# Moving a pair's products behind a step's first product, and x's forms one step behind the norm

## Chip, cores, metric

One core of a Trainium2 chip. The metric is device time in microseconds, the median of several executions. A trace records the clock granted to TensorE. Up to the last matmul it is 1.00 except in stretches of 3.41 us, or two of them in a row, at 0.50; these are called half-clock windows here, and cold windows in the recorded texts.

## The reference

Linear attention on 8 batches x 8 heads x 576 x 64, an RMS norm, then a two-layer block on 4608 tokens with 512 inputs and 2048 hidden units:

```
kv  = einsum('bhsd,bhse->bhde', k, v)
out = einsum('bhsd,bhde->bhse', q, kv)
x   = out / sqrt(mean(out*out, -1) + 1e-6) * g_norm     # -> (4608, 512)
h   = x @ w_in
g   = h * erf(softplus(h))
y   = g @ w_out
```

## The kernel before

Tokens go in groups of 512. The first two groups use plain fp32 matmuls while the weights are brought into fp32 (group 0) and cut into three forms (the "upper" one made by ScalarE, the two "lower" ones by VectorE) that are stored to HBM (group 1). That takes the first 280 us. The other groups use the three forms, and there TensorE is full. The first two groups make 32 steps; step n makes one 128-row slice of h (`h_ps`, 4 matmuls, each run as two) and projects the slice of step n - 5 (`o_ps`). The attention of the next group is cut into pieces, four steps to a pair of heads, and dealt out over the steps. In the traces VectorE, ScalarE and TensorE's matmuls run in the order of the program.

```python
def products():                      # cut
    kv_ps = ...                      # 12 matmuls of k and v; VectorE copies them to bd (block-diagonal)
    qt_ps = ...                      # 4 transposes of q
    nc.scalar.copy(st["qT"], qt_ps)
def apply():                         # cut
    nc.tensor.matmul(kv_ps[:, o_tail], lhsT=bd, rhs=tail, ...)
    nc.tensor.matmul(o_ps, lhsT=bd, rhs=qT, ...)          # se_ps in the profile
    nc.scalar.activation(qT, o_ps, AF.Square)
def halve(): ...                     # VectorE: square into two parts
def mean():  ...                     # TensorE 2 matmuls, ScalarE Ln, Exp, Square (2 table loads)
def norm():  ...                     # VectorE, 3 instructions; reads ms_ps, then se_ps
def split(): ...                     # x into 3 forms: ScalarE one ("upper"), then VectorE two
# the four PSUM tiles of a pair share two banks, so norm must free them for the next products

def pieces_of(T):
    steps = [([], []) for _ in range(FC + 1)]
    for p in range(NP):
        *four, norm, split = attention(T, p)
        for i, piece in enumerate(four):
            step = BATCH * p + i
            if T == 1 and p == 0:
                step = min(i + 1, 3)
            late_in = 0
            if T == FIRST and p == NP - 1 and i == 3:
                step, late_in = step - 1, 1
            steps[step][late_in].append(piece)
        if T == FIRST and p == NP - 1:
            steps[FC - 1][0].extend((norm, split))
        else:
            steps[BATCH * p + BATCH][0][:0] = [norm, split]
    return steps

for n in range(FIRST * FC + 1):      # cut
    for piece in steps[f][0]: piece()
    weights()                        # group 0: weight conversion, 2 ScalarE + 5 VectorE instructions
    # VectorE: hs[n-4] *= ss[n-4]  (the gate)
    # TensorE: h_ps;  ScalarE: copy to h, Softplus
    # group 1: VectorE lowers three weight tiles and stores them, ScalarE uppers two more
    # every 4th step: Erf of four slices on ScalarE, with two table loads
    for piece in steps[f][1]: piece()
    # group 1: third weight upper
    project(n - LAG)                 # TensorE: o_ps
```

Of the kernel before, what the change touches and what calls it, by code (L numbers as in the profile page):

```python
# [49 lines left out]
BATCH = 4  # L50
LAG = 5

FIRST = 2
# [4 lines left out]
def kernel(  # L58
# [17 lines left out]
    NP = H // 2  # L76
    KC = DM // P
    FC = DF // P
# [25 lines left out]
    def softplus_table():  # L104
        nc.scalar.preload_act_table_set("softplus")  # L105
# [137 lines left out]
    def weights():  # L243

        w_next("split")
        w_next("join")
        w_next("load")
# [192 lines left out]
    def w_upper(which, f):  # L440

        t = stage.tile([P, 3, G], FP32R, name="w_new", tag="w_new")
        if which == "in":
            x, parts = w_in_sb[:, :, f * P : f * P + P], t.rearrange("p i (c f) -> p i c f", c=KC)
        else:
            x, parts = w_out_sb[:, f, :], t
        upper_w(x, parts[:, 0])
        w_new[which, f] = t, x, [parts[:, i] for i in range(3)]

    def w_lower(which, f):  # L450
        t, x, parts = w_new.pop((which, f))
        lower_w(x, *parts)
        kept = w_kept[which, f] = dram.tile([P, 3, G], FP32, name=f"w_{which}{f}")
        nc.sync.dma_start(out=kept, in_=t.bitcast(FP32))
# [5 lines left out]
    def project(f, g, last):  # L460
        for j in range(J):
            if f == 0:
                o_ps[j] = ps_o.tile([P, DM], FP32, name=f"o_ps{j}", tag=f"o{j}")
            nc.tensor.matmul(  # L464
                o_ps[j],
                lhsT=g[:, j * P : j * P + P],
                rhs=w_out_sb[:, f, :],
                start=(f == 0),
                stop=last,
            )  # L470

    def store(T, j, e):
        if T < B:
            rows = out[T * S : T * S + G, :].rearrange("(p j) f -> p j f", j=J)
            nc.sync.dma_start(out=rows[:, j, :], in_=e)
            return
        for h, side in enumerate((nc.sync, nc.scalar)):
            first_row = (2 * j + h) * S + G
            side.dma_start(out=out[first_row : first_row + R, :], in_=e[h * R : h * R + R, :])
# [3 lines left out]
    def sums():  # L483

        for j in range(J):
            e = es[j] = acc.tile([P, DM], FP32, name="e", tag="e")
            if j % 2:
                nc.scalar.copy(e, o_ps[j])
            else:
                nc.vector.tensor_copy(out=e, in_=o_ps[j])  # L490

    def unit(name):
        return gate.tile([P, G], FP32, name=name, tag=name[0])
# [28 lines left out]
    def load_parts(which, n):  # L522

        pool = w_in_p if which == "in" else w_out_p
        for _ in range(n):
            if w_seq[which]:
                key = w_seq[which].pop(0)
                t = pool.tile([P, 3, G], FP32, name=f"w_{which}_parts", tag="w")
                nc.sync.dma_start(out=t, in_=w_kept[key])
                w_now.setdefault(key, []).append(t)  # L530


    def pieces_of(T):


        steps = [([], []) for _ in range(FC + 1)]
        for p in range(NP):
            *four, norm, split = attention(T, p)
            for i, piece in enumerate(four):
                step = BATCH * p + i  # L540
                if T == 1 and p == 0:

                    step = min(i + 1, 3)
                late_in = 0
                if T == FIRST and p == NP - 1 and i == 3:
                    step, late_in = step - 1, 1
                steps[step][late_in].append(piece)
            if T == FIRST and p == NP - 1:
                steps[FC - 1][0].extend((norm, split))
            else:  # L550
                steps[BATCH * p + BATCH][0][:0] = [norm, split]
        return steps

    to_cut = [(which, f) for which in ("in", "out") for f in range(FC)]
# [2 lines left out]
    for n in range(FIRST * FC + 1):  # L557
        T, f = divmod(n, FC)
        if n == FC:
            early_room.close()  # L560
            late = ctx.enter_context(tc.tile_pool(name="late", bufs=1))
            x_new = ctx.enter_context(tc.tile_pool(name="x_new", bufs=1))
            acc = ctx.enter_context(tc.tile_pool(name="acc", bufs=J))
            stage_room = ctx.enter_context(ExitStack())
            stage = stage_room.enter_context(tc.tile_pool(name="stage", bufs=5))
            x_forms[FIRST] = late.tile([P, 3, KC, G], FP32R, name="x_forms0")
        if T < FIRST:
            if f == 0:
                ends = steps[FC][0] if T else []
                steps = pieces_of(T + 1)  # L570
                steps[0][0][:0] = ends
            for piece in steps[f][0]:
                piece()
        while w_at["join"] < len(w_order) and w_order[w_at["join"]][0] <= n + 1:
            weights()
        done = n - LAG + 1
        if 0 <= done < whole:
            nc.vector.tensor_tensor(out=hs[done], in0=hs[done], in1=ss[done], op=ALU.mult)
        if T < FIRST:
            h_ps = ps_h.tile([P, G], FP32, name="h_ps", tag="h")  # L580
            for c in range(KC):
                nc.tensor.matmul(  # L582
                    h_ps,
                    lhsT=w_in_sb[:, c, f * P : f * P + P],
                    rhs=xT[T][:, c, :],
                    start=(c == 0),
                    stop=(c == KC - 1),
                )
            if n == whole:
                old_h = wide.tile([P, BATCH, G], FP32, name="h", tag="h")  # L590
            h = hs[n] = old_h[:, n - whole] if n >= whole else unit("h_sb")
            s = ss[n] = unit("s_sb")
            nc.scalar.copy(h, h_ps)
            nc.scalar.activation(s, h, AF.Softplus)
            for key in list(w_new):
                w_lower(*key)
            if T == FIRST - 1:
                for key in to_cut[:2]:
                    w_upper(*key)
                if not w_new and stage_room is not None:  # L600
                    stage_room.close()
                    stage_room = None
                    w_in_p = ctx.enter_context(tc.tile_pool(name="w_in_p", bufs=BATCH))
                    load_parts("in", BATCH)
            if f % BATCH == BATCH - 1:
                for i in range(n - BATCH + 1, n + 1):
                    nc.scalar.activation(ss[i], ss[i], AF.Erf)
                softplus_table()
            for piece in steps[f][1]:
                piece()  # L610
            if T == FIRST - 1:
                for key in to_cut[2:3]:
                    w_upper(*key)
                del to_cut[:3]
        if n >= LAG:
            T2, f2 = divmod(n - LAG, FC)
            last = n - LAG in (FC - 1, whole - 1)
            project(f2, hs[n - LAG], last)
            if last:
                sums()  # L620
                if T2 == 0:
                    for j in range(J):
                        store(T2, j, es.pop(j))
# [41 lines left out]
    for m in range(first_batch, batches + 1):  # L665
        T, b = divmod(m, NB)
# [7 lines left out]
        def piece():  # L674
            if todo:
                todo.pop(0)()
# [79 lines left out]
```

## Time and profile before

| | before |
|---|---|
| median | 989.9 us (989.49 to 991.32) |
| span of the profiled run | 991.4 us |
| TensorE busy | 951.9 us, 96% |
| first h_ps to first n_ps ("part one") | 31.19 to 280.01 us, 248.8 us |

n_ps is the first product of the three-form groups. Steps are counted here from the start of their h_ps. The median is of the three runs that there were before the prediction; a fourth moves it to 990.28, which is used below. The profiled execution itself took 993.23 us, longer than any, so this trace is a slow one. The profile lines themselves are shown in the prediction. In them PE is TensorE, PEld its weight loads, DVE VectorE and ACT ScalarE; L and a number is a line of that kernel, so these differ between kernels.

### The profile page before, as it was taken

The page shows a single profiled execution, that of the slowest core. Times are in us where ns is not written, and L with a number is a line of the kernel's source. Part 1 is how long each engine was busy: PE and PEld are TensorE (multiplying, and loading weights), DVE is VectorE, ACT ScalarE, POOL GpSimd, SP SyncE. Part 2 cuts the span into 40 slices and gives each one's busy share as a digit, 9 for nine tenths or more (in the row PEclk, how much of TensorE's full clock was granted, in tenths as well). Part 3 has the DMA queues.
Part 4 walks back from the last instruction along what each step waited for, and adds up shares of the span by engine and source line. Part 5 has one row for each costly group of instructions (what it writes and reads, how often), then busy time and mean ns, then how long its engine had stood idle before and what let it go on. Part 6 is the DMA issues. An engine that isn't in the chain of part 4 may idle for free.

```text
span 991.4 us, 11745 instructions
## 1 busy us (share of the span) xinstructions
PE 951.9 (96%) x4328; PEld 681.5 (69%) x4328; DVE 736.6 (74%) x1047; ACT 618.7 (62%) x822; POOL 2.4 (0%) x10
## 2 busy tenths in 40 slices
PE   6779999989999999999999999999999999989997
PEld 4334444444477878787878787878787787768885
DVE  2887896657368887777777777888777787776666
ACT  3688776676466666666666666666666666665551
POOL 0000000000000000000000000000000000000000
PEclk9899999999999999999999999999999999999998
DMA  9755516679369976998689878977787678657952
GB/s 278 229 165 165 164 40 246 273 300 376 135 225 362 374 267 233 292 374 294 244 256 371 307 269 248 368 298 280 246 331 250 248 264 343 236 204 284 363 203 74
DMA packets 100936, 259.76 MB, mean 262 GB/s; under 512 B 44048, under 2 KB 57360, under 8 KB 100880
## 3 DMA queue, kind: packets, MB, share of 16 engines
q1 hardware_dynamic: 99248, 256.73, 72.4%
q10 hardware_dynamic: 1568, 2.29, 0.8%
q8 instruction: 34, 0.56, 0.2%
q14 instruction: 22, 0.18, 0.1%
q0 software_dynamic: 64, 0.00, 0.0%
HBM read 224.40 MB, written 34.60 MB: 261 GB/s over the span
## 4 chain that ended last, share of the span: by engine, by line
PE 72%; DVE 15%; ACT 7%; DMA 3%; issue 2%; SPq 0%; DVEq 0%; ACTq 0%
PE n_ps L427 34%; PE m_ps L427 17%; PE h_ps L582 7%; PE o_ps L464 6%; DVE h L718 3%; PE se_ps L304 3%; DVE e L412 2%; PE qt_ps L298 2%; PE kv_ps L276 1%; DMA w_out_parts<-w_out 1%; DVE u L344 1%; DVE x L353 1%; DVE u L341 1%; DVE e L407 1%; ACT L105 1%
## 5 line engine op out<-in xcount | busy, mean ns | idle before, releaser
L427 PE MATMUL n_ps<-x_forms,w_in_parts 128*128 128x512 f32 x896 | 234.2, 403 | 3.0 <-ACT x_forms L378 2.8
L427 PE MATMUL n_ps<-w_out_parts,g_forms 128*128 128x512 f32 x928 | 232.7, 393 | 3.0 <-DMA w_out_parts<-w_out 3.0
L427 PEld LDWEIGHTS n_ps<-w_out_parts,g_forms 128*128 128x128 f32 x928 | 175.6, 189 | 41.1 <-DMA w_out_parts<-w_out 3.8
L427 PEld LDWEIGHTS n_ps<-x_forms,w_in_parts 128*128 128x128 f32 x896 | 167.3, 189 | 47.6 <-issue 9.1
L702 ACT ACTIVATE s<-h 128x512 f32<-128x512 f32 x112 | 71.0, 634 | 200.1 <-DVE h L412 200.1
L427 PE MATMUL m_ps<-w_out_parts,g_forms 128*128 128x512 f32 x464 | 125.0, 391 | 0.0
L582 PE MATMUL h_ps<-xT,w_in_sb 128*128 128x512 f32 x256 | 121.2, 617 | 4.0 <-DVE qT L341 2.7
L427 PE MATMUL m_ps<-x_forms,w_in_parts 128*128 128x512 f32 x448 | 120.8, 392 | 0.0
L412 DVE TENSOR_TENSOR h<-m_ps,h 128x512 f32<-128x512 f32 x112 | 77.1, 688 | 50.4 <-ACT h L700 47.1
L381 DVE TENSOR_TENSOR g_forms<-h,g_forms 128x1024 fp32r<-128x1024 f32 x58 | 70.9, 1223 | 46.9 <-ACT g_forms L378 46.6
L464 PE MATMUL o_ps<-w_out_sb,h_sb 128*128 128x512 f32 x224 | 100.5, 592 | 0.0
L427 PEld LDWEIGHTS m_ps<-w_out_parts,g_forms 128*128 128x128 f32 x464 | 87.8, 189 | 18.4
L427 PEld LDWEIGHTS m_ps<-x_forms,w_in_parts 128*128 128x128 f32 x448 | 84.6, 189 | 17.7
L582 PEld LDWEIGHTS h_ps<-xT,w_in_sb 128*128 128x128 f32 x256 | 49.8, 198 | 63.4 <-issue 55.2
L412 DVE TENSOR_TENSOR e<-m_ps,e 128x512 f32<-128x512 f32 x116 | 80.3, 692 | 17.5 <-PE m_ps L427 9.3
L407 DVE SCALAR_TENSOR_TENSOR e<-n_ps,e 128x512 f32<-128x512 f32 x88 | 60.3, 686 | 28.8 <-PE n_ps L427 28.8
L464 PEld LDWEIGHTS o_ps<-w_out_sb,h_sb 128*128 128x128 f32 x224 | 42.5, 190 | 53.2 <-issue 49.5
L700 ACT ACTIVATE h<-n_ps 128x512 f32<-128x512 f32 x112 | 65.6, 586 | 17.3 <-PE n_ps L427 17.2
L382 DVE SCALAR_TENSOR_TENSOR g_forms<-g_forms 128x1024 fp32r<-128x1024 f32 x58 | 71.1, 1225 | 2.0
L378 ACT ACTIVATE g_forms<-h 128x1024 fp32r<-128x1024 f32 x58 | 61.2, 1054 | 10.0 <-DVE h L718 8.5
L718 DVE TENSOR_TENSOR h<-h,s 128x1024 f32<-128x1024 f32 x56 | 65.9, 1219 | 0.0
L105 ACT ACT_TABLE_LOAD x45 | 57.7, 1283 | 0.8
(82 smaller groups left out, 950.8 us busy)
## 6 DMA issues: line engine op xcount, KB each, us to landing
w_out_parts<-w_out SPq DMA_DIRECT2D x116, 768.0 KB, 7.5
w_in_parts<-w_in SPq DMA_DIRECT2D x112, 768.0 KB, 6.5
w_in<-w_new SPq DMA_DIRECT2D x16, 768.0 KB, 4.3
w_out<-w_new SPq DMA_DIRECT2D x16, 768.0 KB, 5.2
k_sb<-in_k_dram SPq DMA_DIRECT2D x29, 288.0 KB, 4.9
v_sb<-in_v_dram SPq DMA_DIRECT2D x29, 288.0 KB, 5.7
q_sb<-in_q_dram SPq DMA_DIRECT2D x32, 256.0 KB, 5.1
w_raw<-in_moe_w_out_dram SPq DMA_DIRECT2D x8, 1024.0 KB, 4.9
```

What stands on the lines that cost most here:

```text
L105: nc.scalar.preload_act_table_set("softplus")
L378: nc.scalar.activation(high, x, AF.Copy, scale=1.0 + 2.0**-13)
L381: nc.vector.tensor_tensor(out=low, in0=x, in1=high.bitcast(FP32), op=ALU.subtract)
L382: nc.vector.scalar_tensor_tensor(out=both, in0=low.bitcast(FP32), scalar=SHIFT, in1=high.bitcast(FP32), op0=ALU.mult, op1=ALU.add,)
L407: nc.vector.scalar_tensor_tensor(out=out_, in0=ps, scalar=scale, in1=out_, op0=ALU.mult, op1=ALU.add)
L412: nc.vector.tensor_tensor(out=out_, in0=ps, in1=out_, op=ALU.add)
L427: nc.tensor.matmul(ps, lhsT=weights(form, k), rhs=moving(form, k), start=(form == forms[0] and k == 0), stop=(form == forms[-1] and k == 3),)
L464: nc.tensor.matmul(o_ps[j], lhsT=g[:, j * P : j * P + P], rhs=w_out_sb[:, f, :], start=(f == 0), stop=last,)
L582: nc.tensor.matmul(h_ps, lhsT=w_in_sb[:, c, f * P : f * P + P], rhs=xT[T][:, c, :], start=(c == 0), stop=(c == KC - 1),)
L700: nc.scalar.activation(h[:, i], n_ps, AF.Copy, scale=SHIFT - 1.0)
L702: nc.scalar.activation(s[:, i], h[:, i], AF.Softplus)
L718: nc.vector.tensor_tensor(out=h[:, part], in0=h[:, part], in1=s[:, part], op=ALU.mult)
```

## The change

The intent is that TensorE has a product to run while VectorE does a pair's norm (which frees the PSUM banks), and that VectorE does not stand for x's first form.

```diff
-        steps = [([], []) for _ in range(FC + 1)]
+        steps = [([], []) for _ in range(FC)]
         for p in range(NP):
-            *four, norm, split = attention(T, p)
-            for i, piece in enumerate(four):
-                ...                                   # steps 4p .. 4p+3, list [0]
-            ...
-                steps[BATCH * p + BATCH][0][:0] = [norm, split]
+            products, apply, halve, mean, norm, split = attention(T, p)
+            f, last = BATCH * p, p == NP - 1
+            steps[f][1].append(products)
+            steps[f + 1][1].append(apply)
+            steps[f + 2][0].append(halve)
+            steps[f + 3 - last][last].append(mean)
+            steps[f + 4 - last][0].append(norm)
+            steps[f + 5 - 2 * last][0].append(split)
         return steps
...
-                ends = steps[FC][0] if T else []
                 steps = pieces_of(T + 1)
-                steps[0][0][:0] = ends
```

More of the change, by code (lines that the diff above doesn't have):

```diff
@@ L533, in pieces_of @@
     def pieces_of(T):
-        steps = [([], []) for _ in range(FC + 1)]
+        steps = [([], []) for _ in range(FC)]
         for p in range(NP):
-            *four, norm, split = attention(T, p)
-            for i, piece in enumerate(four):
-                step = BATCH * p + i
-                if T == 1 and p == 0:
-                    step = min(i + 1, 3)
-                late_in = 0
-                if T == FIRST and p == NP - 1 and i == 3:
-                    step, late_in = step - 1, 1
-                steps[step][late_in].append(piece)
-            if T == FIRST and p == NP - 1:
-                steps[FC - 1][0].extend((norm, split))
-            else:
-                steps[BATCH * p + BATCH][0][:0] = [norm, split]
+            products, apply, halve, mean, norm, split = attention(T, p)
[6 more added lines that the diff above has]
+            steps[f + 5 - 2 * last][0].append(split)
         return steps
```

## The prediction

> **What bounds the kernel now.** I read the page first. TensorE is busy for 96% of the span and holds 72% of the chain that ended last:
>
> ```profile
> PE 951.9 (96%) x4328; PEld 681.5 (69%) x4328; DVE 736.6 (74%) x1047; ACT 618.7 (62%) x822; POOL 2.4 (0%) x10
> PE 72%; DVE 15%; ACT 7%; DMA 3%; issue 2%; SPq 0%; DVEq 0%; ACTq 0%
> ```
>
> The diff touches only the first two groups (plain fp32 matmuls), from the first h_ps product at 31.2 us to about 279 us. Nothing after that is edited, and there the 50 us windows from 300 to 600 us hold PE work in 49.7 of 50 us. So the change can win only what TensorE loses before 279 us. Second view: windows of that part, cut where the TensorE timeline shows holes (columns: stretch, length, busy us of PE, PEld, DVE, ACT, POOL with counts, granted clock, DMA share, GB/s).
>
> ```profile
> 60.00:69.26 9.26, 6.09 (x10) 2.60 (x11) 7.66 (x11) 8.66 (x12) 0.00 (x0) 0.82 0.53 165
> 69.26:140.00 70.74, 70.74 (x221) 32.94 (x220) 57.83 (x75) 51.36 (x64) 0.00 (x0) 1.00 0.44 140
> 140.00:205.00 65.00, 64.93 (x208) 30.32 (x207) 47.88 (x76) 44.09 (x68) 0.00 (x0) 1.00 0.61 242
> 205.00:227.03 22.03, 19.40 (x69) 8.73 (x67) 12.15 (x22) 17.01 (x25) 0.00 (x0) 0.92 0.73 277
> 227.03:280.00 52.97, 52.97 (x178) 24.83 (x177) 25.60 (x43) 33.30 (x48) 0.00 (x0) 1.00 0.53 211
> ```
>
> TensorE is full in 69 to 205 and in 227 to 280 us. There are two holes behind the start, and both also cost clock: (1 - 0.82) x 9.26 = 1.7 us and (1 - 0.92) x 22.03 = 1.8 us. Third view: the timeline of TensorE in each hole (start, length, what, and in brackets the idle time ahead and its releaser).
>
> ```profile
> 53.95 0.92 PE L276 MATMUL kv_ps<-v_sb,k_sb 96*64 96x64 f32 x24 [1.49 <-DVE u L341]
> 55.47 0.66 PE L298 MATMUL qt_ps<-ident,q_sb 128*128 128x128 f32 x4 [0.59 <-DVE xT L353]
> 63.17 1.12 PE L304 MATMUL se_ps<-qT,bd_kv 128*128 128x512 f32 x2 [3.45 <-ACT qT L299]
> 64.13 5.29 PE L582 MATMUL h_ps<-xT,w_in_sb 128*128 128x512 f32 x8
> ...
> 209.75 0.92 PE L276 MATMUL kv_ps<-v_sb,k_sb 96*64 96x64 f32 x24 [0.37 <-DVE u L341]
> 211.27 0.66 PE L298 MATMUL qt_ps<-ident,q_sb 128*128 128x128 f32 x4 [0.34 <-DVE x L353]
> 220.71 0.43 PE L303 MATMUL kv_ps<-qT_last,bd_kv 128*128 128x64 f32 x2 [1.92 <-DVE qT_last L294]
> 222.24 4.95 PE L582 MATMUL h_ps<-xT,w_in_sb 128*128 128x512 f32 x8
> ```
>
> Hole one idles 1.49 + 0.59 + 3.45 = 5.53 us, hole two 0.37 + 0.34 + 1.92 = 2.63 us. The kv_ps and qt_ps waits are for the two PSUM banks that the previous pair's norm still reads (first norm instruction frees one, third the other). The other waits are for ScalarE's qT copy and for the block-diagonal copies on VectorE. Everything else in the two groups, at the same step numbers of the other pairs, shows no wait over 0.1 us. Fourth view: who made those two late. ScalarE around hole one and VectorE around hole two:
>
> ```profile
> 57.74 1.28 ACT L607 ACT_TABLE_LOAD   x1
> 59.03 2.19 ACT L607 ACTIVATE s_sb<-s_sb 128x512 f32<-128x512 f32 x4
> 61.24 1.28 ACT L105 ACT_TABLE_LOAD   x1
> 62.53 0.59 ACT L299 COPY qT<-qt_ps 128x512 f32<-128x512 f32 x1
> 63.02 1.15 ACT L202 ACTIVATE w_e<-w_e,exp_col 128x1024 int32<-128x1024 int32 x1
> ...
> 218.57 0.69 DVE L381 TENSOR_TENSOR x_forms<-x,x_forms 128x512 fp32r<-128x512 f32 x1 [7.36 <-ACT x_forms L378]
> 220.37 0.29 DVE L294 COPY qT_last<-kv_ps 128x128 f32<-128x128 f32 x1
> ```
>
> In hole one ScalarE works without a gap from 48.6 to 69 us: it is the bound there, because no second product runs before step 5 and each step's weight conversion lies on it. In hole two VectorE stands 7.36 us for x's upper form, which ScalarE gives only after the Erf batch; the copies that TensorE needs stand behind it.
>
> **What the skill says.** (1) "TensorE: Matmul & The Clock Gate", section Architectural detail (queue depths), says that ScalarE and VectorE are strict FIFO. The trace agrees: the copy at 220.37 comes only after the form at 218.57, though its kv_ps had been complete since 211 us. So the place of a piece in program order is what the change buys. (2) The same page, Part 1, gives an activity window of 3413 ns and half the clock after an idle one. The trace agrees: the clock losses of 1.7 and 1.8 us are each one half of a 3.41 us window, and h_ps after each hole took 5.29 and 4.95 us instead of 3.60. (3) "ScalarE: Activation LUTs", What ACT_TABLE_LOAD costs, gives about 1283 ns a load; the trace has 1.28 us. The change neither adds nor removes one.
>
> **The change part by part.** No instruction is added or removed; only order changes. For pair p, step f = 4p: products and apply go from ahead of h_ps of steps f, f+1 to behind it; the norm stays ahead of step f+4; x's forms go one step later. The first pair of the first block stood one step late already, so its TensorE order is the same, and nothing moves before step 4 (about 52 us). For the last pair of that block the mean moves from the start of step 15 to the end of 14 and the norm from 16 to 15; the trace shows no stall there to win (149.25 follows 148.86 + 0.33).
>
> Hole one (steps 4 and 5). TensorE: h3 ends 52.3 by start-to-start of 3.43 us, then h4 at once to 55.7 (before, it began at 55.96), then products, whose banks are free at 53.9 and 55.4: the waits of 1.49 and 0.59 are gone. h5 needs the bank of h3, copied at 56.49 + 0.56 = 57.05, so it runs 57.1 to 60.6. Then apply waits for qT. On ScalarE the table load still ends at 62.53, but now the step's weight conversion (start-to-start 1.05 and 0.95), h4's copy (0.61) and Softplus (0.54) stand ahead of the qT copy: 62.53 + 3.15 = 65.68, plus 0.57 and 0.07 of latency: se_ps starts at 66.3, not 63.17. Idle: 66.3 - 60.6, less about 0.3 for the small product, 5.4 us, against 5.53. TensorE then owes one h_ps less than before (3.43): 63.17 + 3.43 - 66.3 = **0.3 us won**, and the longer single hole costs between 0.9 and 2.5 us of clock instead of 1.7. So hole one moves and hardly shrinks: 0.3 +- 0.8.
>
> Hole two (steps 24 and 25). TensorE: project at 205.79 ends 209.2; h24 follows at once to 212.6; products need banks freed at 209.7 and 211.2, so no wait; 1.4 us, then project to 217.5, h25 to 221. Apply is needed at 221. VectorE no longer waits for x's form: the gating product at 213.9 to 214.6, then three weight lowerings of 1.35 us (the third behind its upper at 217.4 to 218.0) to 219.4, then block-diagonal and tail copies to 220.2. ScalarE: the table at 216.09 ends 217.38, one weight upper to 218.0, h24 copy, Softplus and two uppers (0.6, 0.54, 1.13) to 220.3, qT copy to 220.9. Both arrive at or before 221. All 2.63 us of idle and the 1.8 us of clock go: **4.4 us won**. Earlier there is more margin: the form's wait of 7.36 us at step 20 goes too (at 183.92), so the weight lowerings and their stores come 3 to 5 us earlier.
>
> Elsewhere: apply at steps 9, 13, 17, 21 and 29 has h_ps and project, about 7 us, between products and itself, as before. The qT copy comes 2.4 to 3.2 us later on ScalarE but is needed 3.4 us later. At step 9: qT ready near 95.3, needed near 98.8. No new wait. At the end, x's last forms (272 us) lie 7 us ahead of their first use (280). The second part starts earlier by what was won and is full of TensorE work, so the gain reaches the end. Sum: 4.4 + 0.3 = 4.7; 989.9 - 4.7 = 985.2. I take 985.4, leaving a little for the copies that arrive just in time.
>
> **Rivals.** (A) Both holes close: 5.53 + 1.7 + 2.63 + 1.8 = 11.7, to 978. For it: the norm waits do vanish. Against: ScalarE's unbroken row around hole one, which only shorter ScalarE work could shorten. (B) A wait takes the place of the one removed in hole two: the qT copy now stands behind two weight uppers, and uppers have waited for their stage buffer's store for up to 4.8 us (225.95). If the pair of uppers does so at step 24, apply waits 2 to 4 us and the clock falls again: 988 to 990. Against: the waiting uppers were nearly all the third of a step, which stays behind the pieces. (C) The gain is eaten later by a transfer: PE waits 3.0 us in all for w_out_parts in the second part. Those loads start when the first part's room is freed, so they move with it; at worst 2 us is given back: 987. (D) Hole one grows to two cold windows and is longer by some us: 987 to 988, with hole two closed.
>
> **Range and chances.** The main case 985.4; A half-true pulls to 982.5, B to D push to 988.5. A gain of 2% is 19.8 us, more than the 11.7 us that can be lost there at all; a loss of 2% would need four new holes like these. Faster 0.01, same 0.985, slower 0.005.
>
> **What would show it.** Right: no idle ahead of kv_ps and qt_ps at steps 4 and 24; se_ps of the second pair waiting for ACT qT near 61 to 66 us, 5 us in all, with h_ps started near 52 and 57; one cold window near 66 and none near 220; VectorE's waits for x_forms of 7.4 us gone; the second part's n_ps starting near 275.5 instead of 280.0. Wrong: a wait of apply at step 21 or 25 behind w_new, a step 5 without a hole, or the same n_ps start.

## The result, and the profile after

The change runs in 987.35 us (985.76 to 988.52, 4 runs) beside 990.28 us of before (989.9 without its fourth run): ratio 0.9969, 95% interval 0.995 to 0.9988. Ratios are the mean time of one kernel's fast runs over that of the other's of the same rounds, so not quite the ratio of the medians.

The page after, engines and chain:

```profile
PE 948.9 (96%) x4328; PEld 680.2 (69%) x4328; DVE 737.1 (75%) x1047; ACT 617.8 (63%) x822; POOL 2.4 (0%) x10
...
PE 81%; DVE 12%; ACT 5%; DMA 1%; issue 1%; DVEq 0%
```

The instruction counts are the same, and TensorE's share of the chain rose from 72% to 81%. The windows of part one after, cut at the matching places:

```profile
59.97:67.66 7.69, 2.65 (x6) 1.14 (x6) 6.31 (x10) 7.63 (x11) 0.00 (x0) 0.76 0.81 259
67.66:140.00 72.34, 72.34 (x222) 33.71 (x221) 61.80 (x79) 54.65 (x70) 0.00 (x0) 0.98 0.43 140
140.00:205.46 65.46, 65.46 (x208) 30.47 (x207) 47.04 (x75) 43.51 (x67) 0.00 (x0) 1.00 0.67 257
205.46:221.83 16.37, 16.37 (x67) 7.89 (x66) 9.60 (x17) 14.79 (x24) 0.00 (x0) 1.00 0.74 302
221.83:275.00 53.17, 53.17 (x179) 25.03 (x178) 26.86 (x45) 32.67 (x47) 0.00 (x0) 1.00 0.56 211
```

Hole two is gone: the stretch at 205 us is full at clock 1.00. Hole one is still there, and its clock is lower than before (0.76, and 0.98 even in the 72 us behind it). TensorE's timeline after:

```profile
55.33 0.92 PE L276 MATMUL kv_ps<-v_sb,k_sb 96*64 96x64 f32 x24
56.18 0.66 PE L298 MATMUL qt_ps<-ident,q_sb 128*128 128x128 f32 x4
...
65.79 2.08 PE L304 MATMUL se_ps<-qT,bd_kv 128*128 128x512 f32 x2 [4.68 <-ACT qT L299]
67.66 5.18 PE L464 MATMUL o_ps<-w_out_sb,h_sb 128*128 128x512 f32 x8
72.67 3.60 PE L574 MATMUL h_ps<-xT,w_in_sb 128*128 128x512 f32 x8
...
212.42 0.92 PE L276 MATMUL kv_ps<-v_sb,k_sb 96*64 96x64 f32 x24
...
220.74 0.33 PE L303 MATMUL kv_ps<-qT_last,bd_kv 128*128 128x64 f32 x2
```

No bracket stands at step 4 (55.33, 56.18) or at steps 24 and 25 (212.42, 220.74): the norm's waits are gone. The three waits of hole one (1.49, 0.59 and 3.45 us) became one of 4.68 us for the qT copy, behind one of 0.35 us, and the products after it are slow (2.08 and 5.18 us instead of 1.08 and 3.60). The timelines of ScalarE around hole one and of VectorE around hole two, after, show why one hole stayed and the other closed:

```profile
60.74 1.28 ACT L105 ACT_TABLE_LOAD   x1
62.03 1.15 ACT L202 ACTIVATE w_e<-w_e,exp_col 128x1024 int32<-128x1024 int32 x1
...
65.17 0.57 ACT L299 COPY qT<-qt_ps 128x512 f32<-128x512 f32 x1
```

```profile
217.74 0.29 DVE L294 COPY qT_last<-kv_ps 128x128 f32<-128x128 f32 x1
219.64 0.69 DVE L381 TENSOR_TENSOR x_forms<-x,x_forms 128x512 fp32r<-128x512 f32 x1 [1.60 <-ACT x_forms L378]
```

The qT copy now follows the weight conversion on ScalarE (and, in the lines left out, the copy of h and Softplus). On VectorE the copy for the tail product (217.74) now precedes the form (219.64), whose wait fell from 7.36 to 1.60 us.

The two profiled spans differ by 6.9 us (991.4 and 984.5), more than the times. Part one gives 4.7 of it (248.82 and 244.11 us). The rest is not the change's: 0.5 us lie ahead of the first h_ps, and 1.7 us in the second part up to the last matmul (706.93 and 705.19 us), which nobody edited; the clock records of the trace before have three half-clock windows there, those of the trace after two.

### The profile page after: what moved, and what is told of

The parts are those of the page before. It is cut to its first block, busy times and chain, and to the rows that moved or that the text cites. A ratio compares the mean times of both kernels' runs of the same rounds, so it can differ in the third digit from the quotient of the medians.

```text
span 984.5 us, 11738 instructions
## 1 busy us (share of the span) xinstructions
PE 948.9 (96%) x4328; PEld 680.2 (69%) x4328; DVE 737.1 (75%) x1047; ACT 617.8 (63%) x822; POOL 2.4 (0%) x10
## 4 chain that ended last, share of the span: by engine, by line
PE 81%; DVE 12%; ACT 5%; DMA 1%; issue 1%; DVEq 0%
PE n_ps L427 35%; PE m_ps L427 17%; PE o_ps L464 10%; PE h_ps L574 10%; PE se_ps L304 3%; DVE h L710 3%; DVE e L412 2%; PE qt_ps L298 2%; PE kv_ps L276 2%; DVE x L353 1%; DVE u L344 1%; DVE e L407 1%; DVE u L341 1%; PE ms_ps L326 1%; DVE h L412 1%
## 5 line engine op out<-in xcount | busy, mean ns | idle before, releaser
L574 PE MATMUL h_ps<-xT,w_in_sb 128*128 128x512 f32 x256 | 118.0, 604 | 4.0 <-DVE qT L341 2.7
L412 DVE TENSOR_TENSOR e<-m_ps,e 128x512 f32<-128x512 f32 x116 | 80.2, 692 | 18.4 <-PE m_ps L427 10.1
L105 ACT ACT_TABLE_LOAD x45 | 57.7, 1283 | 0.8
```

The lines of the kernel that those rows point to most:

```text
L105: nc.scalar.preload_act_table_set("softplus")
L412: nc.vector.tensor_tensor(out=out_, in0=ps, in1=out_, op=ALU.add)
L574: nc.tensor.matmul(h_ps, lhsT=w_in_sb[:, c, f * P : f * P + P], rhs=xT[T][:, c, :], start=(c == 0), stop=(c == KC - 1),)
```

## The experiments

Stretches from the traces, in us, from start to start of h_ps: "hole one" is step 2 to step 6, "hole two" step 23 to step 26. Steps 0 to 2 are a start that no kernel here edits; it took 13.8 us where the half clock ended at 36 to 37 us, and 15.3 to 16.8 us where it reached into the next products.

| kernel | median | ratio to before (95%) | start | hole one | hole two | part one |
|---|---|---|---|---|---|---|
| before | 990.28 | | 13.8 | 27.72 | 28.11 | 248.82 |
| before_again (one run) | 990.17 | | 15.3 | 27.72 | 26.42 | 248.69 |
| the change | 987.35 | 0.9969 (0.995 to 0.9988) | 13.8 | 28.20 | 23.23 | 244.11 |
| change_again | 987.78 | 0.9974 (0.9962 to 0.9986) | 15.3 | 27.78 | 23.23 | 245.24 |
| forms_later_only | 987.29 | 0.997 (0.9952 to 0.9988) | 13.8 | 27.72 | 23.23 | 243.95 |
| products_behind_only | 997.81 | 1.008 (1.0062 to 1.0098) | 16.8 | 28.59 | 32.59 | 256.91 |
| second_block_only | 984.62 | 0.9939 (0.9925 to 0.9953) | 13.8 | 27.72 | 23.23 | 243.64 |
| second_block_again | 986.24 | 0.9965 (0.9948 to 0.9982) | 13.8 | 27.72 | 23.23 | 243.64 |
| q_copy_on_vector | 983.32 | 0.9918 (0.9901 to 0.9935) | 13.8 | 22.53 | 23.23 | 238.53 |
| second_block_q_on_vector | 979.86 | 0.9902 (0.9888 to 0.9916) | 13.8 | 22.56 | 23.23 | 238.55 |
| forms_later_q_on_vector | 983.25 | 0.9921 (0.9898 to 0.9944) | 16.8 | 23.84 | 23.23 | 243.13 |
| q_on_vector_only | 983.22 | 0.9943 (0.9917 to 0.997) | 16.8 | 23.82 | 26.39 | 246.30 |

All gave correct results. My theory was that hole two is VectorE standing for x's form, and hole one ScalarE's queue, each independent of the other. The rivals were that the place of the products behind the first product is what wins, or that the wait only moves on.

**x's forms later, nothing else** (on the kernel before):

```diff
-                steps[BATCH * p + BATCH][0][:0] = [norm, split]
+                steps[BATCH * p + BATCH][0][:0] = [norm]
+                if p < NP - 1:
+                    steps[BATCH * p + BATCH + 1][0].append(split)
```

> The order of before with one part of the change alone: x's forms one step behind the norm. My theory (hole two is VectorE standing for x's upper form): the wait of 7.4 us of x_forms goes, the 1.92 us of the tail product and the cold window near 220 go, the waits of 0.37 and 0.34 us of kv_ps and qt_ps stay; from the first h_ps to the first n_ps about 248.8 - 3.9 = 244.9 us (the change: 244.1), hole one as before. Time about 3 us under before, within 1 us of the change. Rival (the place behind the first product does it): no gain, 248.8 us and the time of before.

The time is that of the change (0.997 beside 0.9969). TensorE at steps 24 and 25:

```profile
208.76 0.92 PE L276 MATMUL kv_ps<-v_sb,k_sb 96*64 96x64 f32 x24
...
217.09 0.33 PE L303 MATMUL kv_ps<-qT_last,bd_kv 128*128 128x64 f32 x2
```

Neither line has a wait, though products still stand ahead of h_ps. Here I had expected the norm's waits of 0.37 and 0.34 us to stay. They went too: the norm of step 24 came earlier, its first instruction at 206.65 us, not 209.01 (1.8 us earlier counted from the first h_ps). The likely reason, not tested on its own, is that VectorE was no longer held for 7.36 us at step 20 either, so the weight work ahead of the norm came earlier. So this one move closes all of hole two (28.11 to 23.23).

**Products and apply behind, forms as before** (on the change):

```diff
-            steps[f + 5 - 2 * last][0].append(split)
+            steps[f + 4 - last][0].append(split)
```

> The change with x's forms put back to the norm's step. My theory: at step 24 VectorE stands for the form until about 218.5, then forms, a gate product and three lowerings come ahead of the block-diagonal copies, so the tail product at step 25 waits about 4 us and a cold window comes back: 248 to 251 us from first h_ps to first n_ps, so the time of before or 1 to 2 us over it. Rival (placing products behind the first product is what wins): 244 to 245 us and the time of the change.

This is the slowest kernel, 0.8% over before. Its timelines at steps 24 and 25, VectorE and then TensorE:

```profile
225.60 0.69 DVE L381 TENSOR_TENSOR x_forms<-x,x_forms 128x512 fp32r<-128x512 f32 x1 [7.36 <-ACT x_forms L378]
...
231.99 0.29 DVE L294 COPY qT_last<-kv_ps 128x128 f32<-128x128 f32 x1
```

```profile
232.34 0.69 PE L303 MATMUL kv_ps<-qT_last,bd_kv 128*128 128x64 f32 x2 [6.51 <-DVE qT_last L294]
```

VectorE stands 7.36 us for the form as in the kernel before; but now the forms, a gate product and three weight lowerings come ahead of the copies that TensorE needs. I had expected a wait of about 4 us; it was 6.5, and hole two took 32.59 us. Moving the products without moving the forms is therefore a loss here: the sign was as expected, the size too small (7.4 us over before in the medians, for 1 to 2 expected). (3.0 us of this trace's part one are the start, not the edit.)

**The change for group 2's attention alone** (group 1 in the order of before; `old` is the body of before):

```diff
+        if T < FIRST:
+            return old(T)
         steps = ...                      # the change, for T == FIRST
```

> The change for the attention of group 2 alone, that of group 1 in the order of before. My theory (hole one only moves, and its longer idle costs a second cold window): from first h_ps to first n_ps 243.5 to 244.3 us, so no slower than the change, perhaps 0.5 us faster. Rival (closing the waits of 1.49 and 0.59 us at step 4 is worth something): about 246 us, 2 us slower than the change.

> The change for the attention of group 2 alone, once more. Theory: ratio to before about 0.995, within 1.5 us of the change in the same call, part one 243.6 us give or take a cold window (1.7 us). Rival: again some 3 us less than the change.

Part one was 243.64 us in both traces, 0.47 less than the change in a trace with the same start. So the change's new order for group 1 gains nothing: hole one took 27.72 us in the old order and 28.20 and 27.78 us in the new. In time it was 3 us faster than the change in different calls (0.9939 and 0.9969), but side by side the intervals overlap (0.9965 and 0.9974). Whether it is faster by more than the 0.5 us of the traces stays open. The record gives each run's mean granted clock, and (1 - clock) x span averages 8.0 us for its runs and 10.1 for the change's in the same call. So what difference there is seems to lie in the clock; in the traces hole one has one half-clock window in the old order and two in the new.

**The qT copy of group 1's second pair on VectorE** (on the change):

```diff
-            nc.scalar.copy(st["qT"], qt_ps)
+            if T == 1 and p == 1:
+                nc.vector.tensor_copy(out=st["qT"], in_=qt_ps)
+            else:
+                nc.scalar.copy(st["qT"], qt_ps)
```

> The change with one instruction moved: the qT copy of the second pair of group 1 on VectorE instead of ScalarE. My theory (hole one is ScalarE's queue alone): VectorE makes the copy about 62 us, se_ps starts near 62 instead of 65.8, the idle falls from 4.7 us to under 1.2 and no cold window follows: 237 to 239.5 us from first h_ps to first n_ps, some 5 us less than the change and 8 less than before. Rival (VectorE is as full there, or the bank of h_ps is what holds TensorE next): the wait goes to h_ps or o_ps and under 2 us is won.

One instruction of 0.57 us, moved to another engine, took 5.6 us out of part one. The timelines of VectorE and of TensorE:

```profile
60.59 0.69 DVE L300 COPY qT<-qt_ps 128x512 f32<-128x512 f32 x1
```

```profile
61.34 1.12 PE L307 MATMUL se_ps<-qT,bd_kv 128*128 128x512 f32 x2 [0.29 <-DVE qT L300]
...
66.94 3.67 PE L577 MATMUL h_ps<-xT,w_in_sb 128*128 128x512 f32 x8 [1.05 <-DVE w_in_sb L227]
```

The wait fell from 4.68 to 0.29 us, and no half clock followed. The rival was right in a small way: the next bound is VectorE's weight conversion, 1.05 us later.

**The same copy with group 1 in the old order** (the two edits above together):

> The change for group 2 alone, group 1 in the order of before, and the qT copy of group 1's second pair on VectorE. Theory: in the old place VectorE copies qT about 57 us, before its weight work, so se_ps has no wait; the waits for the norm (1.49 and 0.59) stay; idle of hole one 2 to 3 us in all and no cold window: 238 to 240 us from first h_ps to first n_ps, the time of the change with the copy moved (983), give or take 1.5. Rival (the place behind the first product is what lets the copy pay): 241 us or more.

TensorE's timeline at steps 4 and 5:

```profile
53.03 0.92 PE L276 MATMUL kv_ps<-v_sb,k_sb 96*64 96x64 f32 x24 [1.49 <-DVE u L344]
54.55 0.66 PE L298 MATMUL qt_ps<-ident,q_sb 128*128 128x128 f32 x4 [0.60 <-DVE xT L356]
...
58.65 1.08 PE L307 MATMUL se_ps<-qT,bd_kv 128*128 128x512 f32 x2
```

se_ps has no wait, the norm's waits stay as in the kernel before, and the hole is as short as with products behind (22.56 and 22.53 us). This is the fastest kernel by its median, 979.86 us, ratio 0.9902; it beats both before and the change.

**The change and the kernel before once more, for second traces:**

> The changed kernel once more, with the one of group 2 alone beside it on the same chip. The traces gave 244.1 us against 243.6 us from first h_ps to first n_ps, the times of different calls differ by nearly 3 us. Theory (the rest is TensorE's clock windows and the chip, which differ from run to run): ratio to before 0.995 to 0.997, a new trace with the same idle, 244 us give or take 3 us, the difference lying in cold windows. Rival (hole one costs the change more in most runs than in its trace): ratio about 0.997 again and a trace with hole one longer by 2 us or more.

> The kernel before once more, for a second trace: from first h_ps to first n_ps 248.8 us give or take cold windows of 1.7 us; the two holes at the same steps with idle of 5.5 and 2.6 us.

Both traces have the longer start (15.3 us), so they compare with each other: part one 248.69 and 245.24, 3.45 us apart, not 4.71. The ratio of the change, 0.9974, was the rival's (about 0.997) rather than the 0.995 to 0.997 of the theory, but hole one (27.78 us) was not 2 us longer, as that rival had it. What is missing is clock. TensorE at hole two in before_again:

```profile
222.27 0.43 PE L303 MATMUL kv_ps<-qT_last,bd_kv 128*128 128x64 f32 x2 [1.93 <-DVE qT_last L294]
222.54 1.08 PE L304 MATMUL se_ps<-qT,bd_kv 128*128 128x512 f32 x2
223.46 3.60 PE L582 MATMUL h_ps<-xT,w_in_sb 128*128 128x512 f32 x8
```

The idle is the same as in the first trace (1.93 and 1.92 us), but h_ps takes 3.60, not 4.95 us: this time the hole cost no half clock. In q_on_vector_only, which leaves hole two as it was, it did not either (26.39 us).

**Two last ones: forms later with the copy on VectorE, and the copy alone** (both on the kernel before):

> The kernel before with two edits only: x's forms one step behind the norm, and the qT copy of group 1's second pair on VectorE. Theory (these two instructions' places are all there is to win; the place of products is not): from first h_ps to first n_ps 238.6 + 0.3 = 238.9 us if the start has no second cold window, 1.5 more if it has; ratio to before about 0.990 to 0.992. Rival (moving products behind the first product adds its own gain): 2 us or more over the version that moves them for group 2 with the same copy (238.55 us, ratio 0.9902).

> The kernel before with the qT copy of group 1's second pair on VectorE, nothing else. Theory (the two holes are independent, hole one is ScalarE's queue): hole one shrinks as in the other kernels with this copy, 5.1 us, hole two stays with 26.4 to 28.1 us over its three steps: 242 to 244 us from first h_ps to first n_ps, ratio 0.994 to 0.996. Rival (TensorE early at hole one comes to a wait later in the part): hole two or a new wait grows by what was won and the ratio stays over 0.998.

Both profiled runs had the longest start (16.8 us) and one half-clock window in hole one, so part one missed the expected figures by 2 to 4 us (no half clock had been expected in hole one). The holes show what was asked: the copy alone takes hole one to 23.8 us and leaves hole two at 26.4; with forms later hole two is 23.23 again. The holes are independent. The times (0.9943, 0.9921) agree, but with intervals that reach 0.997 and 0.9944 they do not rank the two-edit kernel against the one of 0.9902.

## Why the prediction was right, and where it was off

- **Hole one moves and hardly shrinks: right.** With first h_ps 0.5 us earlier in this trace, se_ps started at 65.79 for a predicted 66.3, that is as predicted; by the prediction's own sum the order gave the 0.3 us. The clock took it back: two half-clock windows instead of one, which the text had allowed for (0.9 to 2.5 us). Net -0.5 us in one pair of traces, -0.1 in the other, instead of +0.3. That the copy's place in ScalarE's queue was the cause is shown by the moved copy.
- **Hole two closes: right, and for the named reason.** It is the forms' place (forms_later_only) that does it, and not the products' (products_behind_only). The prediction gave the two norm waits to the products' move; the forms' move alone removes them as well.
- **Its size of 4.4 us: a term mis-sized.** The idle was even a little larger than the sum of the brackets (3.2 us from start to start, 26.42 to 23.23, for a predicted 2.63). But the 1.8 us of clock were counted as certain, and of three traces with this hole only one shows them. So hole two is worth 3.2 or 4.9 us, depending on the run.
- **The sum: right in one pair of traces, partly by luck.** Part one fell by 4.71 us there, for a predicted 4.7. But hole two gave 4.88 (predicted 4.4), hole one -0.48 (0.3), and the other steps 0.3 (nothing): the misses cancel. In the other pair part one fell by 3.45 us. The medians fell by 2.9 and 2.2 us, where 4.5 (from 989.9 to 985.4) was predicted. The timed runs have no trace, but each has its mean granted clock. In the call of change_again, (1 - clock) x span averages 10.1 us over 5 runs of the change and 9.6 over 12 of before; without it the spans average 975.2 and 978.9 us. This is an estimate, as the clock is recorded to 0.001, which is 1 us a run. By it the order saved 3.7 us, give or take 1, close to the idle that the traces lack (3.2 in hole two, 0.5 in hole one). The clock saved nothing: about as much was lost as before, where 1.8 us less was predicted. Another 0.3 us was lost outside the span (2.1 us of a run's time for the change, 1.8 for before), for which no run shows a cause.
- **No new wait elsewhere: right.** The other steps have no wait in the trace after. From n_ps on, the length goes with the half-clock windows in it, and not with the edits: 702.8 us with none, 703.8 to 704.7 with one, 704.9 to 706.0 with two, and 706.9 with the three of the first trace of before.
- **Rivals.** A (both holes close) did not happen, though a one-instruction edit nearly does it. B (qT behind weight uppers) did not either: apply at step 25 has no bracket. C stayed small: TensorE's waits for w_out_parts are 3.6 and 3.1 us in the traces of the change, 3.0 and 2.9 before. D, hole one growing to two cold windows, did happen in both traces of the change, and the medians (987.35, 987.78) lie in the 987 to 988 that D names. But hole one grew by 0.5 us at most, not by "some us" as D had it.

## What to carry to other kernels

In an in-order queue, look for the instruction that waits for another engine and for what stands behind it that a third engine needs: here moving the waiting one back gave all of the win of hole two, and moving the needed ones behind it was a loss. Where an engine's row had no gap around a hole, moving whole pieces only moved the hole; taking one instruction off that row closed most of it. Another order on the row itself was not tried: in before, qt_ps was complete at about 56.1 us, and the qT copy at 62.53 stood behind the Erf batch and its two table loads (57.74 to 62.52). Count a clock penalty behind a short idle as a chance, not as a fixed cost, and take a second trace before pricing it: the second point below shows what decides it.

## What the Trainium skill lacked or had wrong

- "TensorE: Matmul & The Clock Gate", Part 1, gives the cold clock after an idle window and calls the window free-running. It gives no busy share for a window that is only partly idle. The prediction took the trace to agree with the page; the size of the loss agrees, but no wholly idle window stood ahead of either hole's half clock in before. Here one idle of 1.9 us, with 0.7 us some 9 us earlier, brought 3.4 us of half clock in one of three traces; an idle of 4.7 us behind one of 0.35 us brought 6.8 us of it in both traces of the change; 1.49 + 0.59 + 3.45 us with work between brought 3.4 us in all five traces of that order that keep the copy on ScalarE.
- What decides this belongs to the same page and can be worked out from the traces. The half-clock records of one trace lie on a grid of 3.41 us (64.53 and 221.54 us in before are 46 windows apart). Take TensorE's busy share of each window of that grid, with every matmul's drawn end 0.17 us earlier (see the next point). Of the 3209 full-clock windows from 40 to 960 us in the twelve traces, 22 were followed by half clock. Their shares were 0 to 0.46; every window at 0.40 or less was followed, none at 0.48 or more, and in between both occur. So it matters how an idle falls on the grid. That of hole two lay wholly in one window in before (218.13 to 221.54, share 0.39: half clock) and before_again (0.41: none), and over two in q_on_vector_only (0.79 and 0.59: none).
- "Perfetto Trace Analysis", per-engine timelines, says that a matmul's end is estimated. No page gives a size: here eight pipelined h_ps matmuls are drawn 3.60 us long but follow each other after 3.43 us, so each idle time in brackets is some 0.17 us short (the tail product at 220.71 us in before is 2.09 us later than the start-to-start distance allows, and its bracket says 1.92).
- "ScalarE: Activation LUTs", What ACT_TABLE_LOAD costs, adds about 1380 ns of drain to the load of 1283 ns. In the rows here the next ScalarE instruction starts 1.29 us after the load does (61.24 to 62.53 in before), and the one ahead ends 0.02 us before it (59.03 + 2.19): no such drain is seen.
